# A fused attention and feed-forward kernel: the bound of the values crosses partitions by DMA, and feed-forward products are dealt out by their time

## The chip, the cores and the metric

The kernel runs on one core of one Trainium2 chip. The metric is the device time of one execution in microseconds. Before the change three runs took 1112.41, 1111.94 and 1110.14 us: the median is 1111.94. One more execution was profiled; it took 1110.84 us, of which the profile's span covers 1109.0. Times in the trace are counted from the start of that span. A difference of about 0.2% (2.2 us) is what a measurement of this kernel can tell from no change.

## The reference, cut to what matters

There are 8 batches, 12 heads, 448 rows and a head size of 64. Queries and keys are normalised, attention is a softmax over 448 keys, and the result of all heads, 768 columns per token, goes through a feed-forward layer with three input weights, of whose products the largest is kept.

```python
q_n, k_n = (rmsnorm(q, g_q), rmsnorm(k, g_k))          # 8 x 12 x 448 x 64
scores = scale * np.matmul(q_n, k_n.transpose(0, 1, 3, 2))
attn = np.exp(scores - np.max(scores, axis=-1, keepdims=True))
attn = attn / (np.sum(attn, axis=-1, keepdims=True) + 1e-09)
x = np.matmul(attn, v).transpose(0, 2, 1, 3).reshape(3584, 768)
h = np.maximum(np.maximum(x @ w1, x @ w2), x @ w3)     # weights 768 x 768
out = h @ w_out
```

## The kernel before, in words

**Groups, chunks and beats.** The work is cut into 48 groups of two heads (six groups to a batch). The 448 queries of a group are four chunks of 112. The program is written out as beats, twelve to a group: `beat(g, i)` issues, engine by engine, what belongs to beat `i` of group `g`. The order in which instructions stand on each engine is the order in which Python issues them; no scheduler moves them. `later(n, work)` puts a piece of work `n` beats further on, and `tick()` at a beat's end issues what has come due.

**A chunk of softmax** takes three beats. TensorE writes the scores of the next chunk (`scores`, line 541, six products in half precision, one of two PSUM buffers `sc`); VectorE takes the row maxima (L550); ScalarE takes the exponentials in place (L567) and the scaled upper half-precision part of the weights (L643); VectorE takes the lower part (L653), after which that score buffer is free. A DMA transpose issued by SyncE (SP) turns the weights (L663, `pt`), and in beat 7 of the next group TensorE multiplies them with the values (`add_values`, L691, 24 products, `av`). The first six groups (`PLAIN`) do the same in full precision, and have TensorE do the turning.

**The feed-forward part of a batch** is a generator (`ffn`) that is put in a queue when the batch's last attention group is done, and that is consumed during the next six groups. It deals out sections of three TensorE products. First come 18 units of `layer1`, six sections each, three per 128 hidden columns (products 128x448, L720). Then come 6 units (8 for odd batches, which also take the tokens that were left over) of `layer2`, six sections each (products 128x384, L784, line `acc[:, :HW]`). In beat `i` the function `thirds` takes `THIRDS[i]` sections, 25 to a group; what is left after the last group is dealt out two sections per tick. Each unit accumulates in one PSUM buffer of the pool `ps_m` (tag `m`, three buffers that are used in turn by everything that asks for them). When a unit is done, `later(1, ...)` has ScalarE or VectorE read it: `hidden` for the first layer (m, maximum, the two halves of `ht`), `result` for the second (ScalarE, `osb`, L793), and then `store` writes it out by DMA.

**The bound of the values.** Values are scaled per batch by a power of their largest magnitude. `largest_v` takes one column per group (L168); `bound_v(b)`, in beat 1 of group 6b (beat 9 of group 0 for the first batch), reduces the six columns to one number per partition (`v_most`, L491) and calls `largest`, which also serves the weights: after 1 beat `turn` multiplies the column with the identity on TensorE (`marks`, L153) into a `ps_m` buffer; after 2 more `reduce` takes the largest of that row on VectorE (L156); after 2 more `spread` multiplies it with a row of ones on TensorE (`most`, L160) into another `ps_m` buffer; after 2 more `scale` computes `v_down` (L494) and `v_up` (L498) on VectorE. `scale_v` on GpSimd (L505, beat 9) needs `v_up`.

**The weights** are decoded during the first eleven groups by ScalarE and VectorE (L186 to L310), a block every four or eight beats. The last step is the split of the six blocks of `w_out` (`wo_sb`: ScalarE L305, VectorE L310), one block per beat, on which the first products of `layer2` wait.

## Time and profile before

| | |
|---|---|
| median of three runs | 1111.94 us |
| profiled execution, its own time | 1110.84 us |
| its span in the trace | 1109.0 us |
| TensorE busy in the span | 1017.1 us (92%) |
| ScalarE, VectorE, GpSimd busy | 771.2, 755.3, 702.4 us |
| mean granted TensorE clock | 0.967 |

In the profile's lists PE is TensorE's products, PEld its weight loads, DVE is VectorE, ACT ScalarE, POOL GpSimd, and SPq the queue from which SyncE issues DMAs. A row of grouped instructions reads: line, engine, operation, output and inputs by tile name, shapes, count, then the busy time in us and the mean of one in ns, then how long the engine stood idle just before them and what ended that. A row of the timeline reads: start, length, engine, line, what, count, and in brackets the idle time ahead of it. A row of a table by stretches of time reads: the stretch, its length, then the busy time and the count of each engine, and last the granted clock, the DMA share and the rate. Products on TensorE are pipelined, so that the busy time of one (some 350 ns) is longer than the distance from one to the next.

### The profile page before, as it was taken

What the parts mean: (1) busy time and instruction counts of PE and PEld (TensorE: products, weight loads), DVE (VectorE), ACT (ScalarE), POOL (GpSimd) and SP (SyncE); (2) the same over time, 40 slices, a digit from 0 to 9 for tenths busy, and PEclk for the clock granted to TensorE, in tenths of its full rate; (3) what the DMA queues carried; (4) which work ended last, traced back from release to release, by engine and by line L of the source; (5) the groups of instructions that cost most, each with busy time, mean ns of one, the idle gap of its engine ahead of it and who ended that gap; (6) DMA issues with size and microseconds to landing.
All of it is one profiled execution on the core that took longest, in us unless ns stands there. A gap on an engine that the chain in (4) does not pass through costs nothing. (4 is left out here: it accounts for less than half of the span.)

```text
span 1109.0 us, 18435 instructions
## 1 busy us (share of the span) xinstructions
PE 1017.1 (92%) x6184; PEld 500.3 (45%) x6184; DVE 755.3 (68%) x1397; ACT 771.2 (70%) x1767; POOL 702.4 (63%) x805
## 2 busy tenths in 40 slices
PE   4668759887899999999999999999999999999998
PEld 2334334343444444444444444444444444445554
DVE  4799988887667676776677766777677666662210
ACT  4599888767777687777777777777777777773001
POOL 5478888775767767677677675776767767610000
PEclk9697879998999999999999999999999999999999
DMA  5554567955888779777887798777877788564002
GB/s 150 161 164 151 139 175 142 188 118 102 172 147 147 134 153 179 152 142 139 170 149 143 143 164 173 144 137 154 169 142 139 140 173 154 91 106 87 1 1 57
DMA packets 426494, 152.30 MB, mean 137 GB/s; under 512 B 372896, under 2 KB 422048, under 8 KB 426400
## 3 DMA queue, kind: packets, MB, share of 16 engines
q1 hardware_dynamic: 425888, 150.95, 67.4%
q8 instruction: 49, 0.80, 0.3%
q14 instruction: 45, 0.37, 0.1%
q10 hardware_dynamic: 512, 0.18, 0.1%
HBM read 51.97 MB, written 11.01 MB: 57 GB/s over the span
## 5 line engine op out<-in xcount | busy, mean ns | idle before, releaser
L720 PE MATMUL acc<-xt,w_sb 128*128 128x448 f16 x2592 | 515.5, 354 | 2.7 <-DVE ht L744 2.2
L720 PEld LDWEIGHTS <-w_sb 128*128 128x128 f16 x2592 | 244.1, 98 | 260.8 <-issue 48.3
L550 DVE TENSOR_REDUCE sc<-sc 112x2 f32<-112x896 f32 x192 | 209.6, 1092 | 53.3 <-PE sc L541 52.2
L567 ACT ACTIVATE sc<-sc,nm,down 112x448 f32<-112x448 f32 x336 | 234.4, 698 | 11.2
L643 ACT ACTIVATE pp<-sc,rs 112x448 f16<-112x448 f32 x336 | 195.0, 633 | 52.0 <-ACT sc L567 47.4
L653 DVE SCALAR_TENSOR_TENSOR pp<-sc,rs,pp 112x448 f16<-112x448 f32 x336 | 212.9, 675 | 4.4 <-ACT pp L643 3.9
L784 PE MATMUL acc<-wo_sb,ht 128*128 128x384 f16 x864 | 151.9, 328 | 12.0 <-ACT osb L793 7.3
L558 ACT ACTIVATE nm<-sc,down 112x2 f32<-112x2 f32 x192 | 50.9, 265 | 158.2 <-DVE sc L550 157.7
L385 POOL TENSOR_TENSOR ri<-ri,half_neg 128x7 f32<-128x7 f32 x96 | 153.9, 1603 | 8.0
L541 PE MATMUL sc<-kt,qt 64*112 64x448 f16 x1008 | 132.1, 367 | 21.5 <-DVE pp L653 18.6
L749 POOL COPY hx<-ht 128x128 f16<-128x128 f16 x48 | 16.2, 337 | 168.0 <-DVE ht L744 167.6
L784 PEld LDWEIGHTS <-ht 128*128 128x128 f16 x864 | 81.4, 98 | 79.4 <-issue 29.0
L691 PE MATMUL av<-pt,vp 128*64 128x448 f16 x1008 | 109.9, 359 | 0.0
L541 PEld LDWEIGHTS <-qt 64*112 64x112 f16 x1008 | 54.2, 126 | 91.6 <-issue 52.4
L438 POOL TENSOR_TENSOR kp<-kn,kp 128x512 f16<-128x512 f32 x42 | 50.5, 1202 | 67.1 <-ACT kp L432 67.1
L636 DVE TENSOR_SCALAR rs<-sc 112x2 f32<-112x2 f32 x168 | 26.7, 159 | 91.1 <-ACT sc L567 91.0
L519 POOL TENSOR_TENSOR vp<-vr,vp 128x448 f16<-128x448 f32 x42 | 44.5, 1059 | 63.0 <-ACT vp L513 61.3
L691 PEld LDWEIGHTS <-vp 128*64 128x64 f16 x1008 | 50.1, 109 | 54.7 <-issue 29.5
L706 DVE SCALAR_TENSOR_TENSOR xt<-av,xt 128x448 f16<-128x448 f32 x42 | 26.2, 625 | 67.0 <-ACT xt L705 67.0
L370 DVE TENSOR_REDUCE ss<-sq 128x7 f32<-128x448 f32 x96 | 61.0, 637 | 10.4 <-ACT sq L361 6.4
L438 POOL TENSOR_TENSOR qp<-qn,qp 112x512 f16<-112x512 f32 x42 | 48.6, 1156 | 19.2 <-ACT qp L432 19.2
L505 POOL TENSOR_SCALAR vr<-vr,v_up 128x448 f32<-128x448 f32 x42 | 60.4, 1438 | 0.0
(111 smaller groups left out, 1202.6 us busy)
## 6 DMA issues: line engine op xcount, KB each, us to landing
raw<-in_moe_w_dram SPq DMA_DIRECT2D x18, 768.0 KB, 4.3
qr<-in_q_dram SPq DMA_DIRECT2D x48, 224.0 KB, 2.8
vr<-in_v_dram SPq DMA_DIRECT2D x96, 96.0 KB, 2.5
kr<-in_k_dram SPq DMA_DIRECT2D x95, 96.0 KB, 3.0
raw<-in_moe_w_out_dram SPq DMA_DIRECT2D x6, 768.0 KB, 5.1
pt<-pp SPq DMA_TRANSPOSE x168, 4.0
out_dram<-osb SPq DMA_DIRECT2D x8, 336.0 KB, 3.0
out_dram<-osb SPq DMA_DIRECT2D x8, 288.0 KB, 3.6
```

Of the source, the lines that this page charges most:

```text
L370: nc.vector.tensor_reduce(sums[g % 2][:sq.shape[0], KQ[what]], sq, axis=AX, op=ALU.add)
L385: nc.gpsimd.tensor_tensor(out=ri, in0=ri, in1=half_neg[:, at], op=ALU.pow)
L438: nc.gpsimd.tensor_tensor(out=parts[:, 1], in0=n, in1=parts[:, 0], op=ALU.subtract)
L505: nc.gpsimd.tensor_scalar(out=vr, in0=vr, scalar1=v_up[:, g // NP:g // NP + 1], scalar2=None, op0=ALU.mult,)
L541: nc.tensor.matmul(sc[:QP, h, :S], qt[rows, qp, c], kt[rows, kp, KEYS[h]], start=n == 0, stop=n == len(TERMS) - 1,)
L550: nc.vector.tensor_reduce(sc[:QP, 0, S + 8:S + 10], sc[:QP, :, :S], axis=AX, op=ALU.max, negate=True)
L567: nc.scalar.activation(to, sc[:QP, h, :S], AF.Exp, bias=nm[:, h:h + 1], scale=down[:QP], accum_out=total,)
L643: nc.scalar.activation(pp[:, 0, h], sc[:QP, h, :S], AF.Copy, scale=rs[:, h:h + 1])
L653: nc.vector.scalar_tensor_tensor(out=pp[:, 1, h], in0=sc[:QP, h, :S], scalar=rs[:, h:h + 1], in1=pp[:, 0, h], op0=ALU.mult, op1=ALU.subtract,)
L691: nc.tensor.matmul(av[half, :S], vp[rows, group, vpart], pt[rows, 7 * wp + group], start=u == 0 and n == 0, stop=u == 3 and n == len(TERMS ...
L720: nc.tensor.matmul(acc[:, :S], wt[:, wp, c], xs[c][:, xp], start=(c == 0 and n == 0), stop=(c == NCT - 1 and n == 2),)
L784: nc.tensor.matmul(acc[:, :HW], lhs, wo_sb[:, f, wp, half * HW:(half + 1) * HW], start=(f == 0 and n == 0), stop=(f == NFT - 1 and n == 2),)
```

## The change

The change has two parts.

The bound of the values no longer uses `largest`. The column of 128 partial maxima is written by a DMA to a row in device memory (`v_row`, 128 writes of 4 bytes), a second DMA reads that row back into all 128 partitions (`v_wide`, 64 KB into SBUF), and VectorE takes the row maximum of 128x128 numbers in place of the 1x128. The DMAs are issued by SP 2 and 4 beats after `bound_v`, and `scale`, with the reduction in it, 6 beats after (before: 7). The bounds of the weights keep their way over TensorE.

Sections of the feed-forward part are counted by their columns: a section of `layer1` counts 1, one of `layer2` counts 384/448 = 0.857. `thirds` keeps the difference between what is due and what has been dealt, and deals while at least half a section is due. `THIRDS[4]` is 2 in place of 3, so that 24 are due in a group in place of 25. A group that deals only `layer2` gets 28 of its sections.

```diff
+    dram = ctx.enter_context(
+        tc.tile_pool(name="dram", bufs=2, space=bass.MemoryType.DRAM)
+    )
...
+        row = dram.tile([1, P], F32, name="v_row", bufs=2)
+        wide = sb.tile([P, P], F32, name="v_wide", bufs=1)
+
-        def scale(bound):
+        def scale():
+            nc.vector.tensor_reduce(most, wide, axis=AX, op=ALU.max)
             nc.vector.tensor_scalar(
-                out=v_down[:, b:b + 1], in0=bound, scalar1=LEAST, scalar2=1.0 / UP,
+                out=v_down[:, b:b + 1], in0=most, scalar1=LEAST, scalar2=1.0 / UP,
                 op0=ALU.max, op1=ALU.mult,
             )
             nc.vector.reciprocal(v_up[:, b:b + 1], v_down[:, b:b + 1])

-        largest(most, scale, (1, 2, 2, 2))
+        later(2, lambda: nc.sync.dma_start(out=row.rearrange("o p -> p o"), in_=most))
+        later(4, lambda: nc.sync.dma_start(out=wide, in_=row.broadcast_to([P, P])))
+        later(6, scale)
...
-            yield
+            yield 1.0
         later(1, lambda: hidden(b, acc, hs, ft, j, keep))
...
-            yield
+            yield HW / S
         later(1, lambda: result(b, acc, osb, tk, half))
...
+    owed = [0.0]
+
     def thirds(n):
-        while queue and n:
+        owed[0] += n
+        while queue and owed[0] >= 0.5:
             try:
-                next(queue[0])
-                n -= 1
+                owed[0] -= next(queue[0])
             except StopIteration:
                 queue.pop(0)
+        if not queue:
+            owed[0] = 0.0
...
-    THIRDS = (2, 3, 2, 2, 3, 2, 2, 0, 2, 2, 3, 2)
+    THIRDS = (2, 3, 2, 2, 2, 2, 2, 0, 2, 2, 3, 2)
```

Line numbers after the change are higher by 3 ahead of `bound_v` and by 10 behind it.

How instructions moved is shown at three places. The first is SP's queue in group 30, where the bound of batch 5 is taken. Before (`pt<-pp` turns softmax weights, `kt` and `qt` keys and queries, `vr` loads values, `out_dram` stores):

```order
L663 DMA_TRANSPOSE pt<-pp 128x14x112
L448 DMA_TRANSPOSE kt<-kp 128x8x128
L448 DMA_TRANSPOSE qt<-qp 128x8x112
L340 DMA vr<-in_v_dram 128x192 x2
L344 DMA vr<-in_v_dram 64x64
L345 DMA vr<-in_v_dram 64x64
L663 DMA_TRANSPOSE pt<-pp 128x14x112
L759 DMA out_dram<-osb 96x768
```

After:

```order
L673 DMA_TRANSPOSE pt<-pp 128x14x112
L508 DMA v_row<-v_most 128x1
L451 DMA_TRANSPOSE kt<-kp 128x8x128
L451 DMA_TRANSPOSE qt<-qp 128x8x112
L343 DMA vr<-in_v_dram 128x192 x2
L347 DMA vr<-in_v_dram 64x64
L348 DMA vr<-in_v_dram 64x64
L673 DMA_TRANSPOSE pt<-pp 128x14x112
L509 DMA v_wide<-v_row 128x128
L769 DMA out_dram<-osb 96x768
```

The first transfer stands ahead of the transposes of keys and queries, the second behind the transpose of the group's first weights. Between the two stand seven other transfers.

The second place is VectorE in the same group, in beats 3 to 9. Before:

```order
L156 TENSOR_REDUCE top<-marks 1x1
L370 TENSOR_REDUCE ss_84<-sq 112x8
L550 TENSOR_REDUCE sc<-sc 112x2
L653 SCALAR_TENSOR_TENSOR pp<-sc,rs,pp 112x448 x2
L636 TENSOR_SCALAR rs<-sc 112x2
L640 RECIPROCAL rs<-rs 112x2
L494 TENSOR_SCALAR v_down<-most 128x1
L498 RECIPROCAL v_up<-v_down 128x1
```

After:

```order
L373 TENSOR_REDUCE ss_86<-sq 112x8
L560 TENSOR_REDUCE sc<-sc 112x2
L663 SCALAR_TENSOR_TENSOR pp<-sc,rs,pp 112x448 x2
L646 TENSOR_SCALAR rs<-sc 112x2
L650 RECIPROCAL rs<-rs 112x2
L500 TENSOR_REDUCE v_most<-v_wide 128x1
L501 TENSOR_SCALAR v_down<-v_most 128x1
L505 RECIPROCAL v_up<-v_down 128x1
```

The reduction of the row has gone from beat 4, and the wider one stands where `v_down` stood; it now waits for a transfer where `v_down` waited for TensorE.

The third place is TensorE at the end of batch 0's first layer, at the scores of beat 2 in group 11. Here `wo_sb` holds the six split blocks of `w_out`, and the number behind `ht` tells the blocks apart: `ht_1685` (after: `ht_1682`) goes with the first block, `ht_1884` (`ht_1881`) with the second, `ht_2423` with the fifth. Before, the rows around the place:

```order
L784 MATMUL acc_2600<-wo_sb_95,ht_2423 128x384
L784 LDWEIGHTS ht_1685
L784 MATMUL acc_2649<-wo_sb_95,ht_1685 128x384
L541 LDWEIGHTS qt_2458
L541 MATMUL sc_2659<-kt_2439,qt_2458 112x448
L784 LDWEIGHTS ht_1884
L784 MATMUL acc_2649<-wo_sb_95,ht_1884 128x384
```

After:

```order
L794 MATMUL acc_2631<-wo_sb_97,ht_1682 128x384
L794 LDWEIGHTS ht_1881
L794 MATMUL acc_2631<-wo_sb_97,ht_1881 128x384
L551 LDWEIGHTS qt_2442
L551 MATMUL sc_2643<-kt_2425,qt_2442 112x448
L794 LDWEIGHTS ht_2070
L794 MATMUL acc_2631<-wo_sb_97,ht_2070 128x384
```

Rows that repeat are left out in both. Before, the products with the first five blocks of `w_out` stand ahead of these scores; after, only those with the first two do, and the third to fifth follow behind them.

## The prediction

> **What bounds the kernel now.** I read the page first, then busy time by stretches cut at the value products (one group each), then the chain of waits, then TensorE's own groups.
>
> ```profile
> span 1109.0 us, 18435 instructions
> PE 1017.1 (92%) x6184; PEld 500.3 (45%) x6184; DVE 755.3 (68%) x1397; ACT 771.2 (70%) x1767; POOL 702.4 (63%) x805
> ```
>
> TensorE is the busiest engine, but 92% is a mean over unlike stages. The stretches part them: the two rows from 319.5 and 918.4 are first-layer groups, those from 398.8 and 518.4 deal second-layer sections alone, the one from 419.9 a mix, and the one from 254.1 is where the second layer first meets the weight decoding.
>
> ```profile
> core 0: us, PE busy (x) PEld busy (x) DVE busy (x) ACT busy (x) POOL busy (x), PEclk, DMA share, GB/s
> 254.10:280.20 26.10, 21.41 (x124) 9.91 (x123) 20.83 (x38) 20.08 (x41) 15.16 (x18) 0.87 0.54 97
> 319.50:339.40 19.90, 19.90 (x124) 9.42 (x123) 13.62 (x28) 13.75 (x33) 13.42 (x18) 1.00 0.75 128
> 398.80:419.90 21.10, 19.05 (x130) 9.93 (x131) 15.59 (x30) 16.85 (x41) 16.13 (x20) 1.00 0.76 155
> 419.90:439.00 19.10, 18.94 (x126) 9.56 (x125) 11.97 (x25) 14.58 (x35) 12.62 (x16) 1.00 1.01 193
> 518.40:539.70 21.30, 18.99 (x130) 9.81 (x129) 14.28 (x29) 16.14 (x40) 14.65 (x19) 1.00 0.83 151
> 918.40:1013.00 94.60, 94.60 (x597) 46.40 (x597) 61.03 (x120) 66.64 (x156) 44.16 (x53) 1.00 0.64 110
> ```
>
> A first-layer group is TensorE from end to end, 19.90 us busy of 19.90. A second-layer group takes longer, 21.10 and 21.30 us, although its products are narrower, and TensorE idles 2.05 and 2.31 us in it. The chain that ended last gives the true prices, since there the products stand back to back:
>
> ```profile
> 918.46 2.51 PE av L691 x24
> 920.96 0.70 PE sc L541 x6
> 921.67 4.08 PE acc L720 x21
> 1001.11 12.29 PE acc L784 x75
> ```
>
> So a first-layer product costs 4.08 / 21 = 0.194 us, a second-layer one 12.29 / 75 = 0.164, the values 2.51 a group, the scores 0.70 a chunk. Twenty-five first-layer sections make 75 x 0.194 + 4 x 0.70 + 2.51 = 19.9 us, the measured row. Twenty-five second-layer ones make 12.29 + 5.31 = 17.6, and 21.1 were taken: 3.5 us are lost in each such group. TensorE's groups from 319.5 us to its end say to what:
>
> ```profile
> L720 PE MATMUL acc<-xt,w_sb 128*128 128x448 f16 x2215 | 437.5, 353 | 0.0
> L784 PE MATMUL acc<-wo_sb,ht 128*128 128x384 f16 x756 | 130.9, 326 | 7.3 <-ACT osb L793 7.3
> L541 PE MATMUL sc<-kt,qt 64*112 64x448 f16 x822 | 106.2, 363 | 5.1 <-DVE pp L653 5.1
> L691 PE MATMUL av<-pt,vp 128*64 128x448 f16 (+1 forms) x864 | 92.8, 356 | 0.0
> L784 PE MATMUL acc<-wo_sb,hx 128*128 128x384 f16 x144 | 24.6, 326 | 0.0
> L153 PE MATMUL marks<-ident,v_most 128*1 128x128 f32 x10 | 1.9, 270 | 0.0
> ```
>
> In these 784.7 us TensorE's own work is 2215 x 0.194 + 900 x 0.164 + 822 x 0.117 + 864 x 0.105 = 764 us. The 20.5 above that are what the change can reach here: idle time of 7.3 + 5.1 = 12.4, and 8.1 of other things.
>
> **Part one, the bound without TensorE.** Eight bounds lose their two steps on TensorE, five of them in the stage above. Their price is the distance they put between other products:
>
> ```profile
> 890.79 1.15 PE L784 MATMUL acc<-wo_sb,ht 128*128 128x384 f16 x6
> 892.18 2.12 PE L784 MATMUL acc<-wo_sb,ht 128*128 128x384 f16 x12
> 895.61 0.65 PE L784 MATMUL acc<-wo_sb,ht 128*128 128x384 f16 x3 [1.30 <-ACT osb L793]
> 896.89 2.12 PE L784 MATMUL acc<-wo_sb,ht 128*128 128x384 f16 x12
> 899.25 2.58 PE L691 MATMUL av<-pt,vp 128*64 128x448 f16 x24
> ```
>
> Six products need 0.98 us, and the next start 1.39 after the first: `marks` costs 0.41. Twelve need 1.97, and the next start after 2.36: `most` costs 0.39. Five times 0.80 is **4.0 us** given back. The wait of 1.30 at 895.61 goes too: `marks` and `most` take two of the turns of the three `ps_m` buffers, so a second-layer unit that starts between them gets the buffer of the unit two before it, not three, and ScalarE has not read that yet. All 7.3 us of that wait lie beside these tiles; without them a unit's buffer has a whole unit (six sections, about 4 us of beats) more to be read.
>
> What the new path adds is a wait of VectorE for `v_wide`, with the row maxima of the next chunk queued behind it, and for those TensorE's scores. In group 30 these rows stand around the place:
>
> ```profile
> 658.32 1.47 SPq L663 DMA_TRANSPOSE pt<-pp  x1
> 660.46 0.14 DVE L494 TENSOR_SCALAR v_down<-most 128x1 f32<-128x1 f32 x1
> 662.75 1.10 DVE L550 TENSOR_REDUCE sc<-sc 112x2 f32<-112x896 f32 x1 [1.94 <-PE sc L541]
> ...
> 903.59 1.27 DVE L653 SCALAR_TENSOR_TENSOR pp<-sc,rs,pp 112x448 f16<-112x448 f32 x2
> 905.99 0.78 PE L541 MATMUL sc<-kt,qt 64*112 64x448 f16 x6
> ...
> vr<-in_v_dram SPq DMA_DIRECT2D x96, 16.0 KB, 2.1
> vr<-in_v_dram SPq DMA_DIRECT2D x96, 96.0 KB, 2.5
> DMA to landing us min/median/max: 3.7/4.0/7.9
> ```
>
> SP gets to `v_wide` behind that transpose, at about 659.8. Loads of 16 and 96 KB, themselves issued behind transposes of keys and queries, land after 2.1 and 2.5 us, so 64 KB should land near 662.2. VectorE would be there at 660.4 and has nothing to do until 662.75: hidden, with 0.5 us to spare. Behind that TensorE has room too: at the same place of group 42 the buffer is free at 904.86, and the scores that want it start 1.1 us later. No row shows a write of 4-byte pieces such as `v_row`; the nearest is the small load of 2.1 us. Seven transfers stand between it and `v_wide`, three of them transposes at 1.47 us of SP's time, so it has over 4 us, and up to that its price is nothing; a slower one would count with the late `v_wide` below. The 128x128 reduction costs VectorE what the 1x128 did, both reading 128 numbers per lane. In the first two bounds VectorE has no such idle time: I take 0.7 us in all, and 0 to 3 as its bounds (a wait of one landing, shared by the two). That TensorE no longer waits for `v_most` there I count at nothing: VectorE's decoding of the weights sets that stage's pace.
>
> **Part two, sections by their time.** A second-layer group now has 28 sections: 84 x 0.164 + 5.31 = 19.1 us of TensorE. A first-layer group has 24: 19.3. Work is only moved; what is won is idle time. Of the three chunks' distances that were short of what softmax needs (7 sections, 0.70 + 21 x 0.164 = 4.14 us), two get 7.5 to 8 sections and reach 4.4 to 4.6. The third, beats 2 to 4, keeps 7. So of the 5.1 us on `pp` I let 3 us stay, 0.6 for each of five second-layer stretches.
>
> The price stands in beat 4 of every first-layer group: the scores of beat 5 come three products, 0.58 us, sooner, and must wait for L653 to release their buffer. The distance before:
>
> ```profile
> 853.78 1.27 DVE L653 SCALAR_TENSOR_TENSOR pp<-sc,rs,pp 112x448 f16<-112x448 f32 x2
> 855.64 0.77 PE L541 MATMUL sc<-kt,qt 64*112 64x448 f16 x6
> ```
>
> The buffer is free at 855.05, the scores start at 855.64: 0.59 us of room, against 0.58 taken. Groups repeat in a few patterns, and this is among the tighter ones; I take 2 us over some thirty groups (bounds 0, and 6 at 0.2 each).
>
> The third piece is the start of the second layer in batch 0:
>
> ```profile
> 261.43 0.78 PE L541 MATMUL sc<-kt,qt 64*112 64x448 f16 x6
> 270.47 1.76 PE L784 MATMUL acc<-wo_sb,ht 128*128 128x384 f16 x5 [2.19 <-DVE wo_sb L310]
> 272.16 1.37 PE L541 MATMUL sc<-kt,qt 64*112 64x448 f16 x6
> 277.46 0.78 PE L541 MATMUL sc<-kt,qt 64*112 64x448 f16 x6
> ...
> PE acc L784 <- DVE wo_sb L310: 3.4, 3, 2.2
> PE acc L784 <- ACT wo_sb L305: 1.2, 2, 0.8
> ```
>
> TensorE waits 4.6 us for weight blocks, and the scores stand behind five of them. After the change they stand behind two and can start some 5 us sooner. But VectorE, 20.83 of 26.10 us busy there, sets the pace of the blocks, so I count **2 us** (bounds 0 and 4.6).
>
> The scores at 272.16 take 1.37 us where those at 277.46 take 0.78, and the clock granted in that stretch is 0.87. The Trainium skill, "TensorE: Matmul & The Clock Gate", section "What's actually happening", says that about 3.4 us of idling halves TensorE's clock until it has been busy as long; the slow scores behind the waits agree. By that rule a removed wait would also give back the slowed products, up to 0.13 x 26.1 = 3.4 us (an estimate), and the time to 1094. I leave it out, since the third to fifth blocks will still be waited for.
>
> **The sum.** Later stage: -4.0 (bound) - 12.4 (idle) - 1.5 (of the other 4.1 us, the refilling of the pipeline behind each wait) + 3.0 + 2.0 = -12.9. Batch 0: -2.0. VectorE's early waits: +0.7. Together -14.2, against the profiled execution's own 1110.84: 1096.6. The median of the runs shown, 1111.94, is 1.1 above that execution, so runs should give 1097.7; I say **1097 us**.
>
> **The rivals.**
>
> *More comes back* (12%): no new wait in beat 5, none on `pp`, and batch 0 gives 4.6 and keeps its clock. Then -4.0 - 12.4 - 1.5 - 4.6 = -22.5: 1089. For it speaks that most groups have over 1 us of room; against it that a tight one has 0.59.
>
> *Softmax is the real bound* (13%): the shortened distance isn't met, first-layer groups stay at 19.9 us and some 20 of them lose the 0.58 that their sections gave up. That returns 11.6 of the 14.2: 1109 for runs; with half of them 1103. Against it: stretches where TensorE has less work, such as 419.9 to 439.0, run at 19.1 us a group.
>
> *The dealing does not cure the second layer* (8%): more sections per beat ask for buffers sooner, the waits for `osb` stay, and only the 4.0 us of the bound and 2 of batch 0 come back: 1107. ScalarE at 16.85 of 21.10 us speaks for it, the tiles beside each such wait against.
>
> *`v_wide` comes late* (9%, the slower side): it is held behind the transpose ahead of it on SP's queue. Transposes land after 4.0 us, at most 7.9. At 7.9, `v_wide` is there at 666.2, 3.5 us after VectorE's idle time ends; TensorE has 1.1 us of room behind that, so it loses 2.4 in five bounds, and 3 in three early ones without cover: 21 us, and 1118. Up to a landing 4 us after its issue it costs nothing; from about 5.6 us all eight together take the 14 us of gain, and the kernel is slower. The Trainium skill's "DMA: Bandwidth & Descriptors", section "Queues, rings and completion order", speaks for it: an engine takes descriptors in ring order, and a completion is signalled only after that engine's earlier writes. The loads that land in 2.1 us behind transposes disagree.
>
> **How the numbers follow.** The forecast has 58%, the rivals 42 as given. Its own range is 1092 to 1103; the range over all is 1087 to 1109, which leaves out the late `v_wide` and the worst of the softmax case. A measurement here tells 0.2%, 2.2 us, from no change: faster by more 86%, within 5%, slower 9%.
>
> **What would show it.** Second-layer groups should take 19.2 to 19.8 us with 84 products, without a wait for `osb`; first-layer groups 19.3 to 19.6. New waits of L541 (now L551) for `pp`, all in beat 5, should add up to 0 to 6 us; if they reach 10, the second rival holds. VectorE should show little idle time ahead of the reduction of `v_wide`. The forecast is wrong if the group times stay at 19.9, or if VectorE's wait for `v_wide` passes 4 us.

## The result and the profile after

The changed kernel takes 1161.6 us (median) against 1111.8 before: a ratio of 1.045, 95% interval 1.044 to 1.0465. The forecast was 1097 us, with 9% for a slower kernel. It was wrong in sign, by 65 us.

The page of the changed kernel begins with these two rows, and its list of DMA issues has the two new transfers (KB each, median us from issue to landing):

```profile
span 1158.6 us, 18388 instructions
PE 1022.3 (88%) x6152; PEld 501.6 (43%) x6152; DVE 755.5 (65%) x1397; ACT 773.3 (67%) x1767; POOL 706.0 (61%) x805
...
v_wide<-v_row SPq DMA_DIRECT2D x8, 64.0 KB, 4.4
v_row<-v_most SPq DMA_DIRECT2D x8, 0.5 KB, 10.3
```

TensorE has 32 instructions fewer than before, and yet 5 us more of busy time and 44 us more of idle time (span less busy: 136.3, before 91.9). `v_row`, 512 bytes, takes 10.3 us to land. The view of waits names the place where this comes back (us in all, times, longest):

```profile
DVE v_most L500 <- DMA v_wide<-v_row: 65.7, 8, 11.1
```

That is 8.2 us for each of the eight bounds. Stretches of the changed kernel, cut as before at the value products, show what follows it. The rows from 689.3 and 813.5 hold a bound; those from 541.9 and 669.5 are pure second-layer groups, the one from 753.1 a first-layer group:

```profile
541.90:563.10 21.20, 19.98 (x135) 10.20 (x136) 15.01 (x32) 16.68 (x40) 16.09 (x20) 1.00 1.07 133
669.50:689.30 19.80, 19.61 (x133) 10.29 (x132) 14.43 (x29) 16.73 (x40) 14.88 (x18) 1.00 0.92 158
689.30:714.00 24.70, 20.93 (x128) 10.24 (x127) 12.70 (x28) 15.40 (x38) 13.61 (x17) 0.93 0.93 161
753.10:772.40 19.30, 19.30 (x121) 9.08 (x120) 15.21 (x30) 15.86 (x38) 13.79 (x17) 1.00 0.74 149
813.50:842.40 28.90, 22.00 (x126) 10.23 (x125) 13.31 (x28) 15.09 (x36) 13.57 (x17) 0.82 0.95 145
```

Most groups without a bound take what was forecast for them: 19.3 to 19.6 for the first layer, 19.8 for the second. Five do not: two of the five pure second-layer groups take 21.2 and 21.4 us, no less than before (21.3 and 21.5), and three groups late in a first layer take 20.7 in place of 19.9. In this later stage, groups with a bound take 24.7 to 28.9 us. Part of that is idle time (28.90 - 22.00 = 6.9 us in the last row), part is slower work: the granted clock falls to 0.82 and 0.93 in these two rows, and 126 instructions take 22.00 us. In a version below, in which nothing waits at this place, the 126 of the same group take 19.30 at a clock of 1.00. The Trainium skill, "TensorE: Matmul & The Clock Gate", section "What's actually happening", has TensorE's clock halved after about 3.4 us of idling until it has been busy as long; these rows agree with it.

The order of events, in the group from 689.3. First SP's queue, then VectorE, then TensorE (start, duration, and in brackets the idle time ahead of the row with what ended it):

```profile
683.88 0.88 SPq L508 DMA_DIRECT2D v_row<-v_most  x1
684.87 1.39 SPq L451 DMA_TRANSPOSE kt<-kp  x1
...
689.98 4.01 SPq L673 DMA_TRANSPOSE pt<-pp  x1
694.04 0.58 SPq L509 DMA_DIRECT2D v_wide<-v_row  x1
```

```profile
690.40 0.17 DVE L650 RECIPROCAL rs<-rs 112x2 f32<-112x2 f32 x1
697.42 0.28 DVE L500 TENSOR_REDUCE v_most<-v_wide 128x1 f32<-128x128 f32 x1 [6.85 <-DMA v_wide<-v_row]
...
698.99 1.27 DVE L663 SCALAR_TENSOR_TENSOR pp<-sc,rs,pp 112x448 f16<-112x448 f32 x2
```

```profile
691.81 0.78 PE L551 MATMUL sc<-kt,qt 64*112 64x448 f16 x6
...
700.36 1.37 PE L551 MATMUL sc<-kt,qt 64*112 64x448 f16 x6 [3.77 <-ACT sc L577]
```

`v_row` goes out at 683.88, and `v_wide` only at 694.04, 10.2 us later. VectorE has been ready since 690.57 and stands until 697.42. The row maxima of the chunk whose scores were done at 692.59 stand behind it, and behind those, on VectorE too, the lower weights of the chunk before. They are the last to read the buffer that TensorE's next scores need; they end at 698.99 + 1.27 = 700.26, and the scores start at 700.36. (The row names ScalarE's exponentials of the newer chunk, which run at the same time but in the other buffer.) Of VectorE's 6.85 us, 692.59 - 690.57 = 2.0 are the idle time that the prediction counted on; 4.8 are lost.

The transfers behind `v_row` are late as well. Issues in a stretch of some 8 us around this place, before (first two rows) and after (KB each, median us to landing):

```profile
vr<-in_v_dram SPq DMA_DIRECT2D x2, 96.0 KB, 2.3
...
kt<-kp SPq DMA_TRANSPOSE x1, 4.2
```

```profile
vr<-in_v_dram SPq DMA_DIRECT2D x2, 96.0 KB, 7.0
...
kt<-kp SPq DMA_TRANSPOSE x1, 9.1
```

### The profile page after: what moved, and what is told of

The parts are those of the page before. It is cut to its first block, busy times and chain, and to the rows that moved or that the text cites. A ratio compares the mean times of both kernels' runs of the same rounds, so it can differ in the third digit from the quotient of the medians.

```text
span 1158.6 us, 18388 instructions
## 1 busy us (share of the span) xinstructions
PE 1022.3 (88%) x6152; PEld 501.6 (43%) x6152; DVE 755.5 (65%) x1397; ACT 773.3 (67%) x1767; POOL 706.0 (61%) x805
## 5 line engine op out<-in xcount | busy, mean ns | idle before, releaser
L730 PE MATMUL acc<-xt,w_sb 128*128 128x448 f16 x2592 | 523.4, 358 | 0.0
L794 PE MATMUL acc<-wo_sb,ht 128*128 128x384 f16 x864 | 149.3, 326 | 4.3 <-ACT osb L803 2.5
L701 PEld LDWEIGHTS <-vp 128*64 128x64 f16 x1008 | 49.6, 108 | 56.0 <-issue 29.6
```

The costliest lines, as they stand in the source:

```text
L701: nc.tensor.matmul(av[half, :S], vp[rows, group, vpart], pt[rows, 7 * wp + group], start=u == 0 and n == 0, stop=u == 3 and n == len(TERMS ...
L730: nc.tensor.matmul(acc[:, :S], wt[:, wp, c], xs[c][:, xp], start=(c == 0 and n == 0), stop=(c == NCT - 1 and n == 2),)
L794: nc.tensor.matmul(acc[:, :HW], lhs, wo_sb[:, f, wp, half * HW:(half + 1) * HW], start=(f == 0 and n == 0), stop=(f == NFT - 1 and n == 2),)
```

## The experiments

### Each part alone

`e1_pace` keeps the dealing by time and takes the bound back to TensorE; `e2_bound` keeps the bound by DMA and deals sections as before.

```
# e1_pace, in bound_v
-        later(2, lambda: nc.sync.dma_start(out=row.rearrange("o p -> p o"), in_=most))
-        later(4, lambda: nc.sync.dma_start(out=wide, in_=row.broadcast_to([P, P])))
-        later(6, scale)
+        largest(most, scale, (1, 2, 2, 2))
# e2_bound
-            yield 1.0                  (layer1; layer2: yield HW / S)
+            yield
-    THIRDS = (2, 3, 2, 2, 2, 2, 2, 0, 2, 2, 3, 2)
+    THIRDS = (2, 3, 2, 2, 3, 2, 2, 0, 2, 2, 3, 2)
```

Expected of the first:

> The dealing by time alone; the bound crosses by TensorE as before. Theory (the dealing does what was forecast, the loss is all the bound's): the working's sum without the 4.0 us of the two TensorE steps and without the 0.7 of VectorE's waits, 1111.8 - 11 = about 1101, in any case under 1106, second-layer groups at 19.3 to 19.8 us with 84 products. Rival (the new dealing is itself part of the loss, by the scores of beat 5 that come sooner): 1112 or more.

Measured: 1108.0 us, ratio 0.997 (0.9956 to 0.998). Expected of the second:

> The bound by DMA alone; the feed-forward sections are dealt by their number as before. Theory (the two parts add up): the nine groups around the eight bounds were 62 us longer in the changed kernel than before, so about 1112 + 62 = 1174, or 1168 and more. Rival (the two parts make the loss together, since the new dealing left TensorE no slack to take up a late bound): below 1150.

Measured: 1160.8 us, ratio 1.044 (1.041 to 1.046). That is neither the 1168 or more of two parts that add up nor the less than 1150 of two that make the loss together: beside this bound the dealing makes no difference that can be told (1160.8 against 1161.6). The whole loss is the bound's. The dealing is no part of it, but alone it gives 3.9 us where 11 were expected, and two second-layer stretches of `e1_pace` take 21.2 and 21.9 us, not 19.3 to 19.8. TensorE's groups of `e1_pace` from 316.0 us to its end say what stays (busy us, mean ns, idle time before them with what ended it), to be held against the 7.3 and 5.1 of the kernel before:

```profile
L787 PE MATMUL acc<-wo_sb,ht 128*128 128x384 f16 x756 | 131.0, 326 | 4.1 <-ACT osb L796 2.5 <-DVE ht L747 0.8 <-ACT ht L743 0.6
L544 PE MATMUL sc<-kt,qt 64*112 64x448 f16 x822 | 106.2, 363 | 5.8 <-DVE pp L656 5.8
...
L156 PE MATMUL marks<-ident,v_most 128*1 128x128 f32 x10 | 1.9, 270 | 1.9 <-ACT osb L796 1.9
```

4.1 + 5.8 + 1.9 = 11.8 us of idle time against 12.4. My expectation was careless here: by the prediction's own words the waits for `osb` hang on the turns that `marks` and `most` take, and this kernel still has them. With those 7 us left out, the working would have said 1108, but that would have been luck. The working puts the gain into the later stage, and from the values of group 12 on `e1_pace` takes 790.5 us where the kernel before takes 789.5 (in one profiled execution of each). What it wins lies ahead of that: from the values of group 6 to those of group 12 it takes 131.6 us against 136.5.

### The loss taken apart

`e3_row` adds to `e1_pace` the write of `v_row` at its beat, and nobody waits for it. `e4_row_wide` adds the read of `v_wide` too, so that SP waits for `v_row`; VectorE uses neither. Then the changed kernel differs by VectorE's wait, and by the two tiles on TensorE that it does without.

```
# e3_row: largest(most, scale, (1, 2, 2, 2)) stays, and
+        later(2, lambda: nc.sync.dma_start(out=row.rearrange("o p -> p o"), in_=most))
# e4_row_wide: and
+        later(4, lambda: nc.sync.dma_start(out=wide, in_=row.broadcast_to([P, P])))
```

> The dealing by time, the bound by TensorE, and beside it the write of v_row at its place, for which nobody waits. Theory (the loss is the wait of VectorE for v_wide, the write holds up nothing that matters): as the kernel with the dealing alone, within 3 us. Rival (the write holds back all transfers issued behind it for its 10 us, and the transposes and loads among them are then late for TensorE): 10 us or more above the dealing alone.

> As the one before with the read of v_wide as well, which SP issues when v_row has landed; VectorE uses neither. Theory (VectorE's wait is the loss): within 5 us of the dealing alone, so that 55 us or so remain for the wait of VectorE. Rival (SP stands about 9 us at each of the eight reads, and the transposes behind it are issued that much later): 20 us or more above the dealing alone, with waits of TensorE for kt, qt or pt.

Measured: 1121.2 us (ratio 1.009, 1.007 to 1.011) and 1128.3 us (1.015, 1.011 to 1.019). So the 53.6 us between the dealing alone and the changed kernel are 13.2 for a write that nobody waits for, 7.1 more when SP also reads it back and has to wait for it, and 33.3 more when VectorE waits (less what the two tiles save). The runs of `e4_row_wide` spread from 1123.6 to 1134.0, so the border between the last two is known to some 5 us. Both theories were too simple, and both rivals' numbers held: VectorE's wait is the largest part, and the held transfers a quarter. The waits of `e3_row` show those (of its waits for transfers, this is the one that grew most):

```profile
ACT pp L648 <- DMA pt<-pp: 14.8, 6, 5.3
```

ScalarE cannot write the next `pp` because the transpose that reads the old one lands late; in `e1_pace` that row reads 0.6 us.

### What makes `v_row` slow

Two probes put an extra write, waited for by nobody, into beat 10 of the groups 8 to 47 of `e1_pace`.

```
# e11_probe2 (e5_probe had eight kinds, with 4 pieces of 128 bytes and a write into SBUF)
+    PROBES = (                       # name, numbers a piece, distance, one partition in so many
+        ("p_near", 1, 1, 1), ("p_half", 1, 1, 2), ("p_quarter", 1, 1, 4),
+        ("p_apart", 1, P, 1), ("p_line", 1, 16, 1), ("p_long", 32, 32, 1),
+    )
+        src = ident.rearrange("(p e) n -> p e n", e=every)[:, 0, :n]
+        to = dram.tile([P // every, apart], F32, name=name, bufs=8)
+        nc.sync.dma_start(out=to[:, :n], in_=src)
```

> The dealing alone, with one extra transfer in beat 10 of each group from 8 to 47, which nobody waits for: eight kinds in turn, among them 128, 64 and 32 pieces of 4 bytes to neighbouring places in HBM, 128 pieces of 4 bytes 512 bytes apart, 128 pieces of 128 and of 512 bytes, 4 pieces of 128 bytes, and 128 pieces of 4 bytes into SBUF. Theory (small writes to HBM are paid one by one on each DMA engine, 10.3 us / 8 = 1.3 us a piece of its ring): 128 near 10 us, 64 near 5 to 6, 32 near 3 to 4, whether neighbouring or apart; 128 pieces of 512 bytes and those into SBUF near 2 to 3; 128 of 128 bytes near 10; 4 of 128 near 2 to 3. Rival 1 (pieces that fall into the same 512 bytes of HBM wait for each other): those apart near 2 to 3 us. Rival 2 (the price is the 4-byte read from 128 partitions of SBUF, or the number of pieces): those into SBUF and those of 512 bytes near 10 as well.

Measured: 1123.4 us in a single run. Its profile lacks some of the records of landings, and the list of issues therefore gives no time for any transfer; the second probe has fewer kinds.

> The dealing alone with an extra write to HBM from beat 10 of each group from 8 to 47, six kinds in turn, for which nobody waits: 128 neighbouring pieces of 4 bytes (near), 64 (half), 32 (quarter), 128 pieces of 4 bytes each 512 bytes apart (apart) and 64 bytes apart (line), and 128 neighbouring pieces of 128 bytes (long). Theory (pieces of different DMA engines that fall into the same short stretch of HBM wait for each other): near and half about 10 us, quarter 4 to 7, apart and long 2 to 3; line near 10 if the stretch is 512 bytes, near 2.5 if it is 64 or less. Rival (each small write is paid on its ring): half about half of near, apart and line as near.

Measured: 1138.3 us in a single run, and these landings:

```profile
p_quarter<-ident SPq DMA_DIRECT2D x7, 0.1 KB, 4.4
p_apart<-ident SPq DMA_DIRECT2D x7, 0.5 KB, 2.4
p_line<-ident SPq DMA_DIRECT2D x7, 0.5 KB, 2.4
p_long<-ident SPq DMA_DIRECT2D x7, 16.0 KB, 3.1
...
p_half<-ident SPq DMA_DIRECT2D x6, 0.2 KB, 9.8
```

The list has no time for `p_near`, but that is `v_row` itself, at 10.3. Smallness by itself costs nothing here: the same 128 pieces of 4 bytes, placed 64 bytes apart, land in 2.4 us, like any small load. 128 neighbouring pieces of 128 bytes take 3.1. Of neighbouring pieces of 4 bytes, 64 still take 9.8 and 32 take 4.4. So what costs is that small pieces lie side by side in HBM, as the theory had it, and my guess of a fixed price for each piece is out. Distances of 4, 64 and 512 bytes were tried: how far apart is enough lies somewhere between 4 and 64. Nor is it only how many pieces share 64 bytes: in all three neighbouring kinds there are 16 of them, and 32 pieces land after 4.4 us, 64 and 128 after 9.8 and 10.3. Whether they wait within one DMA engine or across engines, no run told apart. The Trainium skill, "DMA: Bandwidth & Descriptors", section "Specifications", has the DMA engines do a read-modify-write in transfers below 512 bytes; these rows show that this alone is not the price, since `p_line` and `p_half` are both below.

`e16_row_apart` takes this back to the kernel: `e3_row` with one edit, each piece 64 bytes from the last.

```
-        row = dram.tile([1, P], F32, name="v_row", bufs=2)
-        later(2, lambda: nc.sync.dma_start(out=row.rearrange("o p -> p o"), in_=most))
+        row = dram.tile([P, 16], F32, name="v_row", bufs=2)
+        later(2, lambda: nc.sync.dma_start(out=row[:, :1], in_=most))
```

> The dealing alone and, as in the run with the write of v_row for which nobody waits, its 128 pieces of 4 bytes on SP's queue at the same beat, but each to a place 64 bytes from the last. Theory (what holds the transfers is that the pieces share 64-byte stretches of HBM): within 3 us of the dealing alone, 1107 to 1111, and v_row lands after 2.4 us. Rival (a write of 128 small pieces costs its place in the queue, however far apart): near the 1121 of the neighbouring pieces.

Measured: 1108.2 us, ratio 0.997 (0.996 to 0.998): the 13 us are gone, as expected, though `v_row` lands after 3.2 us and not 2.4. In its lists of issues and of waits, `v_row` and the wait that stood at 14.8:

```profile
v_row<-v_most SPq DMA_DIRECT2D x8, 0.5 KB, 3.2
```

```profile
ACT pp L648 <- DMA pt<-pp: 0.5, 1, 0.5
```

`e12_row_actq` asks what is held, SP's queue or the DMA engines: `e3_row` with the write issued by ScalarE.

```
-        later(2, lambda: nc.sync.dma_start(out=row.rearrange("o p -> p o"), in_=most))
+        later(2, lambda: nc.scalar.dma_start(out=row.rearrange("o p -> p o"), in_=most))
```

> The dealing alone and the write of v_row as in the changed kernel, waited for by nobody, but issued by ScalarE's queue and not by SP's. Theory (transfers are held because they stand behind the write in SP's own rings): SP's transfers are not held, so within 4 us of the dealing alone, 1108 to 1112. Rival (the DMA engines themselves are held, for whatever queue): as with the write on SP's queue, about 1121.

Measured: 1124.0 us, ratio 1.012 (1.010 to 1.014). The transposes on SP's queue are held by a write on another queue, as the same two rows show:

```profile
v_row<-v_most ACTq DMA_DIRECT2D x8, 0.5 KB, 9.6
```

```profile
ACT pp L648 <- DMA pt<-pp: 12.2, 5, 3.3
```

By the Trainium skill, "DMA: Bandwidth & Descriptors", section "Queues, rings and completion order", both queues run on the same engines, and an engine signals a completion only after all its earlier writes, whichever queue they came from. The trace agrees. The prediction had named a part of that rule, and set it aside because loads landed fast behind transposes; those transposes had no slow write in them.

### Earlier, or in fewer pieces

`e6_early` begins seven of the eight bounds in beat 9 of the group before. `e8_blocks` stays at the place of the change, but VectorE turns the 128 maxima in blocks of 32 x 32 (0.20 us), so that `v_row` goes out in 4 pieces of 128 bytes. `e9_blocks_early` does both.

```
# e6_early
-            later(4, lambda: largest_v(g + 6))
+            later(3, lambda: largest_v(g + 6))
-        if g > 1 and g % NP == 0 and g < G and i == 1:
-            bound_v(g // NP)                              # v_row, v_wide, scale after 2, 4, 6 beats
+        if g % NP == NP - 1 and g < G - 1 and i == 9:
+            bound_v(g // NP + 1, (1, 7, 10))
# e8_blocks: most is column 0 of a 128 x 32 tile sq, its other columns zero
-        later(2, lambda: nc.sync.dma_start(out=row.rearrange("o p -> p o"), in_=most))
+        def write():
+            nc.vector.transpose(turned, sq)
+            nc.sync.dma_start(
+                out=row.rearrange("o (a r) -> (o a) r", r=32),
+                in_=turned.rearrange("(a r) n -> a r n", r=32)[:, 0],
+            )
+        later(2, write)
```

> The changed kernel with seven of the eight bounds begun four beats earlier (beat 9 of the group before), so that v_row has about 11 us until v_wide is read and that 5 us until VectorE wants it. Theory (33 us are VectorE's wait, 7 SP's, 13 the held transfers): the first two go but for the bound of batch 0, the held transfers stay: 1114 to 1122. Rival (the held transfers are late for the softmax wherever the row is written, and are what VectorE's wait really was): above 1140.

> The changed kernel with one edit: VectorE first turns the 128 maxima in blocks of 32 x 32, so that v_row is written in 4 pieces of 128 bytes in place of 128 of 4. Theory (the pieces are the price): v_row lands in 2 to 3 us, the transfers behind it are not held, VectorE waits under 2 us a bound, and the time is that of the dealing alone less the two TensorE steps of each bound: 1100 to 1106. Rival (the way over HBM with two landings in a row is too long at this place, whatever the pieces): 1125 or more.

> As the one before, with seven bounds begun four beats earlier, two landings of 4.8 us each allowed for. Theory: VectorE's waits go to zero but for the bound of batch 0: 1099 to 1104, under the one before by 0 to 5. Rival (the earlier reduction and transfers fall where VectorE and SP have less room): above the one before.

Measured: 1130.2 us (ratio 1.017, 1.015 to 1.019), 1135.0 us (1.022, 1.020 to 1.023) and 1112.1 us (1.001, 0.9998 to 1.002). All three theories missed; of the rivals that of `e8_blocks` held. In `e6_early` VectorE still waits 23.6 us for `v_wide`, and my edit made a new wait of 22.7 by taking the row maxima of the values one beat nearer to their load. `e8_blocks` is the one to learn from: there the row holds nothing up (the transpose of keys issued right behind the row of the example lands after 3.2 us, not 9.1), and half of the loss is still there. SP and VectorE around one of its bounds:

```profile
668.99 0.56 SPq L516 DMA_DIRECT2D v_row<-v_turned  x1
669.66 1.24 SPq L451 DMA_TRANSPOSE kt<-kp  x1
...
676.19 1.06 SPq L522 DMA_DIRECT2D v_wide<-v_row  x1
```

```profile
674.13 0.17 DVE L663 RECIPROCAL rs<-rs 112x2 f32<-112x2 f32 x1
680.60 0.29 DVE L506 TENSOR_REDUCE v_sq<-v_wide 128x1 f32<-128x128 f32 x1 [6.30 <-DMA v_wide<-v_row]
```

SP waited 1.2 us for VectorE's turned block ahead of the first row; from there on nothing holds it. It has seven other issues to make between the two, and comes to `v_wide` 7.2 us after `v_row`. VectorE is ready at 674.30, `v_wide` goes out 1.9 us after that and is there 4.4 us after its issue. With 2 us of cover the bound loses 4 us, whatever `v_row` costs. `e9_blocks_early` gives SP and VectorE that time, and the wait for `v_wide` is gone, but the other edit costs here too:

```profile
DVE v_rows L171 <- DMA vr<-in_v_dram: 26.3, 15, 3.3
```

`e10_blocks_early2` puts that back and begins the bound in beat 10; `e14_old_dealing` is the same bound with sections dealt as before.

```
# e10_blocks_early2, against e9_blocks_early
-            later(3, lambda: largest_v(g + 6))
+            later(4, lambda: largest_v(g + 6))
-        if g % NP == NP - 1 and g < G - 1 and i == 9:
-            bound_v(g // NP + 1, (1, 4, 7))
+        if g % NP == NP - 1 and g < G - 1 and i == 10:
+            bound_v(g // NP + 1, (1, 4, 8))
```

> As the bound in blocks that is begun early, but the row maxima of values stay in their old beat (there they wait for the load for 26 us) and the bound begins one beat later. Theory (the DMA way costs nothing once SP and VectorE have time for it, and then both parts give what was forecast, since marks and most no longer take turns of ps_m): 1097 to 1103, VectorE's waits for values back at 5 us or less, and no wait of TensorE for osb over 3 us in all. Rival (the added transfers themselves cost the 4 us that TensorE gives up): 1106 to 1110, like the dealing alone.

> The same bound as in the run before it, with the sections dealt by their number as in the kernel before. Theory (the waits for osb hang on the two tiles of the bound, not on the dealing): 1111 - 4 - 5 = about 1102 to 1105, so that the dealing is worth 2 to 4 us with this bound as well. Rival (the waits for osb hang on the dealing): 1107, four under the kernel before, and the dealing worth 7 or more.

Measured: 1110.9 us (ratio 0.999, 0.998 to 1.0003) and 1111.8 us (1.001, 1.0001 to 1.0025). VectorE's waits for `v_wide` are gone, and so is the gain. The theory of the first missed by 8 us and its rival by 1; the second came out 5 above the upper of its two numbers. In `e10_blocks_early2` a new wait stands in the way, behind some bounds and not behind others:

```profile
ACT pp L666 <- DMA pt<-pp: 9.5, 4, 3.7
```

### What is left: SP's queue

Two versions of `e10_blocks_early2` ask whether the transposes are late for the 64 KB of `v_wide` or for SP's two more issues. `e20_four` lets VectorE take the largest of each block, so that 4 numbers cross and `v_wide` is 2 KB; `e15_actq` has ScalarE issue both transfers.

```
# e15_actq
-            nc.sync.dma_start(
+            nc.scalar.dma_start(
                 out=row.rearrange("o (a r) -> (o a) r", r=32),
...
-        later(at[1], lambda: nc.sync.dma_start(out=wide, in_=row.broadcast_to([P, P])))
+        later(at[1], lambda: nc.scalar.dma_start(out=wide, in_=row.broadcast_to([P, P])))
# e20_four
+            nc.vector.tensor_reduce(four, turned, axis=AX, op=ALU.max)
...
-        wide = sb.tile([P, P], F32, name="v_wide", bufs=1)
+        wide = sb.tile([P, 4], F32, name="v_wide", bufs=1)
```

> The bound in blocks, begun early, on SP's queue, where VectorE first takes the largest of each block, so that 4 numbers cross and v_wide is 2 KB in place of 64. Theory (it is SP's issue time): no better than with 64 KB, 1109 to 1112. Rival (it is the 64 KB): 1102 to 1107.

> The bound in blocks, begun early, with both of its transfers issued by ScalarE and not by SP. Theory (SP's queue is nearly full where the bound falls, and the two issues make the transposes behind them late): no wait of ScalarE for a transpose longer than 2 us behind a bound in groups 18 and 30, and 1102 to 1107. Rival 1 (the 64 KB of v_wide themselves hold the transposes): as with SP, 1109 to 1112. Rival 2 (ScalarE, 15.5 of 19.4 us busy there, has no room for the issues): 1112 or more.

Measured: 1111.0 us (ratio 1.000, 0.999 to 1.001) and 1103.5 us (0.993, 0.9915 to 0.9945). It is not the bytes; it is SP's queue. Both theories held, and the rivals with them are out. With ScalarE issuing, the same row of waits reads

```profile
ACT pp L666 <- DMA pt<-pp: 2.0, 2, 1.1
```

and the groups around the bound stand level. Of `e15_actq`, groups 36 and 18, then of `e10_blocks_early2` groups 18 and 19:

```profile
775.70:795.00 19.30, 19.30 (x126) 9.43 (x127) 12.38 (x27) 14.19 (x34) 12.45 (x16) 1.00 0.95 186
419.50:438.90 19.40, 19.40 (x129) 9.73 (x130) 12.76 (x28) 15.45 (x37) 13.64 (x17) 1.00 0.96 191
```

```profile
417.00:437.10 20.10, 19.49 (x127) 9.71 (x126) 13.04 (x28) 15.83 (x39) 14.01 (x17) 1.00 0.98 181
437.10:458.70 21.60, 19.50 (x120) 9.35 (x120) 13.45 (x27) 13.47 (x32) 13.30 (x18) 1.00 0.94 164
```

`e15_actq` is faster than the kernel before and than `e1_pace`. Whether SP lacks the time to issue or the order within its rings decides was not tried apart.

### The dealing, with nothing in its way

`e21_actq_old_dealing` is `e15_actq` with the sections dealt by their number, the edit of `e2_bound`.

> The best kernel so far (bound in blocks, begun early, issued by ScalarE, 1103.5) with the sections dealt by their number as before. Theory (with TensorE free of the two tiles of the bound, the waits for osb go with either dealing, and the dealing only moves work): 1103 to 1106, the dealing worth 0 to 2 us. Rival (the dealing is worth what was forecast for it, 12.4 + 1.5 - 5.0 = 8.9 in the later stage): 1110 or more.

Measured: 1106.6 us, ratio 0.996 (0.994 to 0.997), so the dealing is worth 3.1 us by the medians, with intervals that touch; both numbers lie just above the theory's, and the rival's 1110 is out. Two pure second-layer groups of it, to be held against 21.10 and 21.30 of the kernel before with the same 75 products:

```profile
398.20:417.20 19.00, 18.16 (x126) 9.64 (x127) 14.13 (x28) 15.69 (x38) 14.03 (x17) 1.00 0.78 164
516.60:536.30 19.70, 18.07 (x124) 9.50 (x123) 13.28 (x28) 15.34 (x37) 12.95 (x17) 1.00 0.83 159
```

And TensorE's idle time in the later stage, first with the old dealing (from 318.9 us), then with the new (`e15_actq`, from 320.3):

```profile
L807 PE MATMUL acc<-wo_sb,ht 128*128 128x384 f16 x756 | 129.2, 326 | 1.9 <-ACT osb L816 1.9
L564 PE MATMUL sc<-kt,qt 64*112 64x448 f16 x822 | 106.2, 363 | 8.2 <-DVE pp L676 8.1
```

```profile
L807 PE MATMUL acc<-wo_sb,ht 128*128 128x384 f16 x756 | 130.6, 326 | 4.1 <-ACT osb L816 2.5 <-DVE ht L767 1.0 <-ACT ht L763 0.6
L564 PE MATMUL sc<-kt,qt 64*112 64x448 f16 x822 | 106.1, 363 | 6.1 <-DVE pp L676 6.1
```

10.1 us against 10.2. In this stage the dealing moves idle time from one wait to another and removes none; the 3.1 us do not lie there. Cut at the values of group 6 and of group 12, the two executions show where they lie. First the old dealing, then the new:

```profile
183.00:318.90 135.90, 117.07 (x704) 55.40 (x703) 107.56 (x200) 101.04 (x227) 96.58 (x105) 0.95 0.73 145
318.90:1102.00 783.10, 768.09 (x4801) 379.22 (x4800) 498.21 (x983) 528.80 (x1235) 471.11 (x569) 1.00 0.70 133
```

```profile
188.10:320.30 132.20, 114.12 (x706) 54.79 (x707) 106.49 (x195) 98.52 (x220) 97.21 (x106) 0.97 0.72 145
320.30:1105.50 785.20, 770.17 (x4804) 379.31 (x4803) 497.79 (x983) 530.03 (x1234) 469.91 (x567) 1.00 0.69 133
```

The new dealing wins 3.7 us in the six groups in which the first batches' sections meet the decoding of the weights, and loses 2.1 in the later stage. The other two pairs agree: 4.9 won and 1.0 lost beside the bound on TensorE, 2.5 won and 2.3 lost beside that on SP's queue (`e14_old_dealing`, `e10_blocks_early2`). Of what is lost, some 0.6 are three products that the new dealing leaves over for the later stage. What lies ahead of group 6 differs by some 6 us among these six executions, though dealing begins only in its last 20 us, so for the whole the medians decide. Nor does the bound on ScalarE's queue come free everywhere: the stretch from 673.4 of `e21_actq_old_dealing`, beside a bound, takes 22.0 us.

## Why the prediction was wrong, point by point

**The price of `v_row`: the step that failed.** The prediction took a write of 4-byte pieces at the 2.1 us of the nearest row, a load of 16 KB, and said that up to 4 us its price is nothing. It measured 10.3. That load was the smallest row to be had, but of another kind: it reads pieces of 256 bytes from HBM, where this writes 128 pieces of 4 bytes side by side. The range for an operation that no row shows reached from 2.1 to "over 4", and nothing in the trace set its upper end.

**What a slow transfer does to others.** The prediction let a slow `v_row` count with the late `v_wide` alone. Such a write also makes transfers behind it land late, whichever of the two queues issued it: 13.2 us by itself (`e3_row`, `e12_row_actq`; gone in `e16_row_apart`).

**`v_wide` hidden in 1.94 us of idle time: failed by itself.** The idle time is there, 2.0 us. But `v_wide` lands after some 4.4 us, not the 2.4 of the working; the trace of before had a hint at the very place, a store of 288 KB issued at 659.89, just where `v_wide` would go, which landed after 3.7. And SP's own 0.88 us for `v_row`, ahead of the transpose of keys, was left out of the time at which it reaches `v_wide`. `e8_blocks`, with a cheap row, still takes 1135.0. The three early bounds, for which 0.7 stood in the sum, cost some 20: up to the values of group 12 the changed kernel takes 337.6 us, `e1_pace` 316.0 (this part differs by some 6 us among executions whose bound costs little).

**The rival on the slower side** named the right wait and the right chain behind it, and asked for 3.5 us of lateness at the transposes' longest landing. Its cause was wrong (the transfer is held by `v_row`, and SP reaches it late), its size was 21 us of loss where the bound cost 53.6, and its 9% too little for a sum that rested on a price no row showed. The prediction's own mark, a wait of VectorE over 4 us, is passed by each bound on average (8.2).

**The two steps on TensorE: right in the main.** Without them pure second-layer groups with the old dealing go from 21.10 to 19.00 and from 21.30 to 19.70 us (`e21_actq_old_dealing`), and the waits for `osb` from 7.3 to 1.9. The turns of `ps_m` were as said, but not for all of the 7.3: what stays are two waits of 0.94, each about 1 us ahead of `marks` in the kernel before. The 0.80 of a bound fits, and no run shows it by itself.

**Sections by their time: right in most groups, wrong in the sum.** First-layer groups of 19.3 to 19.6, three second-layer groups of 19.8 with 84 products, and 5.8 us of waits for `pp` against 5.0 forecast; but two second-layer groups stay above 21 us, and three first-layer groups get longer. The failed term is "-12.4": it was all put down as gone, less those 5.0. What the two tiles held back, 5.4, went with the tiles and not with the dealing; and where the sections of the second layer follow one another faster, waits for `osb` and `ht` of 4.1 came back, which is the third rival in part. For the later stage 8.9 were forecast of the dealing, and it lost 1.0 to 2.3. In batch 0 it won 2.5 to 4.9 where 2.0 were forecast, and not where they were looked for: the stretch in which the second layer first meets the decoding went from 26.1 to 25.7 us in `e1_pace`, and to 25.7 with the old dealing in `e21_actq_old_dealing` as well; the two stretches before it together went from 49.6 to 47.5 in `e1_pace`. Why these got shorter stays open. By the medians the dealing gave 3.9 beside the bound on TensorE, 3.1 beside that on ScalarE's queue, and 0.9 beside that on SP's.

**The clock in batch 0.** The prediction read the slow scores at 272.16 as agreeing with a clock that halves after about 3.4 us of idling. No single wait ahead of them is longer than 2.19, and the granted clock had already gone to half at 267.65, before that one. The rows with a bound, where TensorE idles 3.77 and 6.9 us at a stretch, are the better witnesses.

## What to carry to other kernels

When no row of the trace shows an operation, the nearest row must be near in kind (direction, piece size, how the pieces lie), and the chance of the slow side must be worked out from what waits for it. Price a new transfer in four places: its landing, its issue time in a queue that is already full, what lands late behind it, and who waits on the reading side. And before a wait is put down to how work is dealt out, look at which tiles take turns beside it. When a variant comes out faster, cut both traces at the same places and see in which stage the time was won.

## What the runs showed of the hardware

Writes to HBM of 64 and 128 pieces of 4 bytes landed after 9.8 and 10.3 us where the pieces lie side by side, and those of 128 after 2.4 where each lies 64 or 512 bytes from the next (3.2 in `e16_row_apart`). Transfers issued behind such a write landed late: a transpose after 9.1 us in place of 4.2, loads of 96 KB after 7.0 in place of 2.3. With the write on ScalarE's queue, the transposes on SP's still kept ScalarE waiting for 12.2 us in place of 0.6. Reading one row of 512 bytes into 128 partitions took a median of 4.4 us in the changed kernel, 3.9 in `e15_actq` and 5.0 in `e21_actq_old_dealing`, where the loads of 96 KB took 2.6, 2.4 and 2.4; with a row of 16 bytes it took 3.2.
